# K and Q projections that write PSUM in pair order, flat copies out of PSUM, and a refitted order

## The chip, the cores and the metric

The kernel runs on one core of a Trainium2 chip. The metric is the device time of one execution in microseconds (us). The executions of one kernel mostly agree within 1%. Where a ratio is given, it is the mean time of one kernel's fast runs over the mean of the other's of the same rounds, so it is not quite the ratio of the medians quoted beside it. Of each kernel one execution was profiled.

In the profiles PE is TensorE (matmuls), PEld its weight loads, ACT ScalarE, DVE VectorE and POOL GpSimd.

## The reference, cut to what matters

```python
# x: (1, 2048, 512) bf16; 64 segments of 32 tokens, 8 memory rows carried from one to the next
for s in range(64):
    h = concat([mem, x_norm[s*32:(s+1)*32]])          # 40 rows
    q, k, v = h @ Wq, h @ Wk, h @ Wv                  # each 512 -> 32 heads x 128
    p = softmax(mask(q @ k.T * 128**-0.5))
    o = (p @ v) @ Wo                                  # 32*128 -> 512
    mem, out[s] = o[:8], o[8:]                        # the next segment needs these 8 rows
# then a residual, two layernorms and an MLP 512 -> 1792 -> 512 over all 2048 rows
```

## The kernel before: the parts that matter

The projections run as four column tiles of 32 side by side. Matmul `j` of a group writes the 512 results of 16 heads, columns `32*j` to `32*j+31` of each head, into 32 partitions of a PSUM bank. Four groups (`cc`) add up over the 512 inputs. The 32 rows are the 24 first tokens and the 8 memory rows of a segment (`hT`, "segment rows"), or the 8 last tokens of each of four segments together (`hB`, "block rows").

```python
def one_pass(lhs, reads, W, key, r, bank, rhs):
    for cc in range(DC):
        def f(e, cc=cc):
            for j in range(4):
                ins = e.matmul(ps[bank][32 * j:32 * j + 32, :], lhs(cc), rhs(W, r, cc, j), start=(cc == 0), stop=(cc == DC - 1), tile_position=(0, 32 * j))
            return ins
        S.op("pe", f, reads=[(key, r, cc)] + reads, writes=[("ps", bank)], dur=0.216, mode=MC, ni=8)

def cols_kq(W, r, cc, j):
    return W[:, cc, r * 2048:(r + 1) * 2048].rearrange("p (h e) -> p h e", h=16)[:, :, 32 * j:32 * j + 32]

def kq_out(i, bank, scale_=None):            # copy out of PSUM, to bf16
    src = ps[bank][:, :].rearrange("p (h b e) -> p h b e", b=2, e=32)
    dst = pairs(kqP[:, i, :]).rearrange("p h e b -> p h b e")
    S.either(copy2(dst, src, 512, True, scale_), reads=[("ps", bank)], writes=[("kqP", i)])

def pair_T(dst, i, key):                     # two bf16 heads transposed as one 4-byte word
    S.op("dve", lambda e: e.transpose(dst.bitcast(U32), kqP[:, i, :].bitcast(U32)), ...)
```

PSUM holds head pair `h`, head `b`, column `e` in that order. The transpose on DVE wants the two heads of a pair side by side, so the copy on ACT reads PSUM flat and writes bf16 at a step of two elements. What follows is a chain: K and Q transposed, eight Q columns copied into ZC, the score matmuls (line 771), softmax, PV, the output projection (line 884), and `hT`, the memory rows of the next segment. `ORDER` and `BANKS` give the PE order and the PSUM banks, tuned for each position of a segment in its block of four. `BONUS`, `LEAN` and the `dur=` numbers steer where a scheduler places the work of ACT, DVE and POOL at build time.

## Time and profile before

| | before |
|---|---|
| time | 877.5 us |
| busy share of the span: PE / ACT / DVE | 93% / 71% / 60% |
| PE busy between 200 and 700 us | 487.7 of 500 us |
| start to start, four K/Q column tiles of 128x512 | 216 ns (median) |
| copies of K and Q: 160 casts, 160 scaled | 740 and 757 ns |
| copies of V, same size, not stepped | 586 ns |
| period of a segment | 11.16 us |

The period is the mean distance of the transposes of `TT`, one for each segment, over 52 segments of the steady part; the start-to-start times are worked out from the starts of the matmul records.

From the page of the kernel before: the engine row (busy us, share, instructions) and the chain that ended last, by engine and by line.

```profile
PE 813.7 (93%) x22285; PEld 444.2 (51%) x22045; DVE 529.0 (60%) x1651; ACT 626.7 (71%) x1624; POOL 145.5 (17%) x353
...
PE 70%; DVE 12%; ACT 11%; DMA 3%; issue 2%; SPq 1%; POOL 0%; DVEq 0%
```

The groups of instructions of the kernel before (line, engine, operation, out<-in, shapes, count | busy us, mean ns of one | idle time of the engine just before, and what ended it):

```profile
L619 PE MATMUL ps<-WQ,hT 128*32 128x512 bf16 x2048 | 154.8, 383 | 4.7 <-DVE hT L890 4.6
L619 PE MATMUL ps<-WK,hT 128*32 128x512 bf16 x2048 | 152.4, 379 | 0.0
L619 PE MATMUL ps<-WV,hT 128*32 128x512 bf16 x2016 | 147.3, 380 | 0.0
...
L645 ACT ACTIVATE kqP<-ps 128x512 bf16<-128x512 f32 x160 | 119.4, 757 | 28.6 <-PE ps L619 27.2
L644 ACT CAST kqP<-ps 128x512 bf16<-128x512 f32 x160 | 117.0, 740 | 13.3 <-PE ps L619 10.9
...
L644 ACT CAST VS<-ps 128x512 bf16<-128x512 f32 x128 | 74.8, 586 | 2.6 <-PE ps L619 1.4
...
L771 PEld LDWEIGHTS ps<-KALL,ZC 128*32 128x32 bf16 x2048 | 25.8, 96 | 58.1 <-DVE KALL L672 51.3 <-ACT ZC L641 1.4 <-DVE QT L672 0.9
```

K, Q and V matmuls are alike, about 380 ns each. That is the recorded duration of one, whose end the profiler models; four run side by side, and a new four start every 216 ns. The K and Q copies are 154 to 171 ns longer than the V copies of the same size. The last line is the weight load for the scores: it sat idle for 51 us in all until K had been copied and transposed, but part of that idle time is hidden behind matmuls that still run. The true gaps are seen in the matmul starts: between 130 and 750 us, the gaps before the score matmuls exceed the undisturbed 216 ns by about 16.5 us in total.

One steady stretch of the chain of waits (start us, us, what):

```profile
438.91 3.48 PE ps L619 x64
442.40 0.25 PE ps L771 x13
```

64 column tiles are 16 groups of four, at 3.48 / 16 = 0.2175 us each: here the chain is nothing but PE at its rate.

### The profile page before, as it was taken

To read this page: it belongs to the slowest core of one execution; us is meant where nothing else is said; L and a number is where in the kernel's file an instruction comes from. 1 tells how busy PE (TensorE), PEld (TensorE's weight loads), DVE (VectorE), ACT (ScalarE), POOL (GpSimd) and SP (SyncE) were. 2 spreads that over 40 slices of the span, in tenths; PEclk is the share of its full clock that TensorE was granted. 3 is DMA by queue.
4 is the path that set the end of the run, shared out by engine and by line. 5 is a ranking of instruction groups with operands and counts; after the bars stand their busy time and mean duration, and the time that the engine had idled before them with its cause. 6 is when DMAs were issued, how large, how long until landed. Compare 5 with 4: busy or idle time off the path is not lost.

```text
span 878.3 us, 48583 instructions
## 1 busy us (share of the span) xinstructions
PE 813.7 (93%) x22285; PEld 444.2 (51%) x22045; DVE 529.0 (60%) x1651; ACT 626.7 (71%) x1624; POOL 145.5 (17%) x353
## 2 busy tenths in 40 slices
PE   2478999999999999999999999999999998899998
PEld 0134555555555555555555555555555554544443
DVE  2146666767676767676767676767676767442111
ACT  1348887878787878787878787878787877644442
POOL 3022111212120212121212111111111111033200
PEclk9879999999999999999999999999999999999999
DMA  8860001010101010101010101010101110501000
GB/s 339 303 210 16 4 7 31 13 32 10 35 10 29 17 28 16 28 16 29 16 28 16 28 16 28 10 28 10 28 11 28 34 28 10 198 34 49 24 25 25
DMA packets 35305, 40.48 MB, mean 46 GB/s; under 512 B 2452, under 2 KB 31004, under 8 KB 35100
## 3 DMA queue, kind: packets, MB, share of 16 engines
q1 hardware_dynamic: 35100, 37.38, 13.0%
q8 instruction: 174, 2.85, 1.3%
q14 instruction: 31, 0.25, 0.1%
HBM read 28.98 MB, written 8.39 MB: 43 GB/s over the span
## 4 chain that ended last, share of the span: by engine, by line
PE 70%; DVE 12%; ACT 11%; DMA 3%; issue 2%; SPq 1%; POOL 0%; DVEq 0%
PE ps L619 30%; PE ps L884 16%; PE ps L1162 6%; PE quad L1169 6%; PE quad L801 3%; ACT kqP L645 3%; ACT EC L783 2%; PE ps L771 2%; ACT kqP L644 2%; PE ps L631 2%; PE ps L830 2%; PE quad L856 1%; DVE PC L789 1%; PE ps L396 1%; DVE opT L912 1%
## 5 line engine op out<-in xcount | busy, mean ns | idle before, releaser
L619 PE MATMUL ps<-WQ,hT 128*32 128x512 bf16 x2048 | 154.8, 383 | 4.7 <-DVE hT L890 4.6
L619 PE MATMUL ps<-WK,hT 128*32 128x512 bf16 x2048 | 152.4, 379 | 0.0
L884 PE MATMUL ps<-WO,OT 128*32 128x256 bf16 x4224 | 141.6, 275 | 6.2 <-ACT OT L644 3.2
L619 PE MATMUL ps<-WV,hT 128*32 128x512 bf16 x2016 | 147.3, 380 | 0.0
L645 ACT ACTIVATE kqP<-ps 128x512 bf16<-128x512 f32 x160 | 119.4, 757 | 28.6 <-PE ps L619 27.2
L644 ACT CAST kqP<-ps 128x512 bf16<-128x512 f32 x160 | 117.0, 740 | 13.3 <-PE ps L619 10.9
L884 PEld LDWEIGHTS ps<-WO,OT 128*32 128x32 bf16 x4224 | 96.1, 96 | 35.9 <-ACT OT L644 17.7
L644 ACT CAST OT<-quad 128x128 bf16<-128x128 f32 (+1 forms) x192 | 85.4, 445 | 36.6 <-PE quad L805 32.9
L845 POOL TENSOR_TENSOR PA<-SA,rsa 128x256 bf16<-128x256 f32 x64 | 40.1, 627 | 379.5 <-DVE rsa L844 263.2
L896 DVE STREAM_TRANSPOSE TT<-ps 128x256 f32<-128x256 f32 x66 | 29.7, 450 | 107.3 <-PE ps L884 107.1
L619 PEld LDWEIGHTS ps<-WQ,hT 128*32 128x32 bf16 x2048 | 57.0, 97 | 59.4 <-DVE hT L890 13.9
L672 DVE STREAM_TRANSPOSE KALL<-kqP 128x256 uint32<-128x256 uint32 x160 | 70.1, 438 | 26.4 <-ACT kqP L644 24.1
L619 PEld LDWEIGHTS ps<-WK,hT 128*32 128x32 bf16 x2048 | 57.8, 97 | 54.3 <-ACT kqP L645 6.4
L783 ACT ACTIVATE EC<-ps,nmc 128x64 f32<-128x64 f32 x256 | 77.9, 309 | 8.7 <-DVE nmc L779 8.7
L1165 ACT ACTIVATE WQ<-ps,b1t 128x512 bf16<-128x512 f32 x56 | 38.5, 688 | 61.4 <-PE ps L1162 60.9
L644 ACT CAST VS<-ps 128x512 bf16<-128x512 f32 x128 | 74.8, 586 | 2.6 <-PE ps L619 1.4
L672 DVE STREAM_TRANSPOSE QT<-kqP 128x256 uint32<-128x256 uint32 x128 | 56.7, 443 | 21.9 <-ACT kqP L645 18.8
L842 ACT ACTIVATE SA<-SA 128x256 f32<-128x256 f32 x64 | 26.5, 414 | 45.3 <-DVE SA L841 43.6
L771 PEld LDWEIGHTS ps<-KALL,ZC 128*32 128x32 bf16 x2048 | 25.8, 96 | 58.1 <-DVE KALL L672 51.3
L1169 PE MATMUL quad<-WK,WQ 128*128 128x512 bf16 x224 | 54.4, 379 | 0.5 <-DVE xr L930 0.5
L1213 DVE TENSOR_TENSOR WV<-quad,WV 128x512 bf16<-128x512 f32 x16 | 11.1, 691 | 65.9 <-PE quad L1169 65.8
L642 POOL COPY ZC<-QT 128x128 bf16<-128x128 bf16 x112 | 33.0, 295 | 104.3 <-DVE QT L672 103.6
(111 smaller groups left out, 1282.3 us busy)
## 6 DMA issues: line engine op xcount, KB each, us to landing
WV<-in_A_Wv_dram SPq DMA_DIRECT2D x4, 1024.0 KB, 6.7
WK<-in_A_Wk_dram SPq DMA_DIRECT2D x4, 1024.0 KB, 8.0
v_last<-VSB SPq DMA_DIRECT2D x64, 64.0 KB, 2.1
WQ<-in_A_Wq_dram SPq DMA_DIRECT2D x4, 1024.0 KB, 8.0
VBD<-v_last SPq DMA_DIRECT2D x64, 64.0 KB
WO<-in_A_Wo_dram SPq DMA_DIRECT2D x4, 1024.0 KB, 8.9
WK<-in_B_w_dram SPq DMA_DIRECT2D x2, 1792.0 KB, 13.0
xr<-in_A_x_dram SPq DMA_DIRECT2D x16, 128.0 KB, 2.9
```

The costliest lines, as they stand in the source:

```text
L619: ins = e.matmul(ps[bank][32 * j:32 * j + 32, :], lhs(cc), rhs(W, r, cc, j), start=(cc == 0), stop=(cc == DC - 1), tile_position=(0, 32 * j))
L642: "pool": (lambda e: e.tensor_copy(out, src), t_pool(n))}
L644: return {"act": (lambda e: e.copy(out, src), t_act(n, ps_)), "dve": (lambda e: e.tensor_copy(out, src), 0.165 + 1.0e-3 * n * fast)}
L645: return {"act": (lambda e: e.mul(out, src, scale_), t_act(n, ps_)), "dve": (lambda e: e.tensor_scalar(out, src, scale_, None, ALU.mult), ...
L672: S.op("dve", lambda e: e.transpose(dst.bitcast(U32), kqP[:, i, :].bitcast(U32)), reads=[("kqP", i)], writes=[key], dur=0.445)
L771: ins = e.matmul(ps[bank][32 * j:32 * j + 32, 64 * sl:64 * sl + 64], ZC[:, par, h, :], rhs, start=False, stop=(i == 3), tile_position=(0, ...
L783: ins = e.activation(EC[:, r, sl, :], ps[bank][:, 64 * sl:64 * sl + 64], ACTF.Exp, bias=nmc[:, r, sl:sl + 1], accum_out=smc[:, r, sl:sl + 1])
L845: pa = lambda e: e.tensor_tensor(PA[:], SA[:], bc(rsa), ALU.mult)
L884: ins = e.matmul(ps[bank][32 * j:32 * j + 32, 0:256], lhs(slot(h)), wo_cols(h, b), start=(k == 0), stop=(k == 15), tile_position=(0, 32 * ...
L1162: ins = e.matmul(ps[bank][:, 0:SBT], W1[:, cc, fc * P:(fc + 1) * P], hnT_of(k)[:, cc, :], start=(cc == 0), stop=(cc == DC - 1))
L1165: S.op("act", lambda e: e.activation(gT[:, fc, :], ps[bank][:, 0:SBT], ACTF.Gelu_apprx_tanh, bias=b1t[:, fc:fc + 1], scale=1.0), reads=[(" ...
L1169: S.op("pe", lambda e: e.matmul(quad[:, t, :], gT[:, fc, t * P:(t + 1) * P], W2[:, fc, :], start=(fc == 0), stop=(fc == FC - 1)), reads=[" ...
```

## The change

The intent: let the PE put the two heads side by side, so that the copy on ACT is flat on both sides and no longer pays for its step. Three parts: the PSUM pattern of the K and Q matmuls, the flat copy, and newly fitted `ORDER`, `BANKS`, `BONUS`, `LEAN` and some `dur=` entries. The cut diff:

```diff
-BONUS = {"EC0": -2.26, "EC1": 40, ...          # all values new
+BONUS = {"EC0": 7.93, "EC1": -1.44, ...
-LEAN = 22.363
+LEAN = 15.318
-(("Q0", 0, 2), ("K0", 0, 3), ("Q0", 2, 4), ("Q1", 0, 1), ("K0", 3, 4), ("Q1", 1, 4), ("K1", 0, 4), ("SC0", 0, 1), ("V0", 0, 2), ...
+(("Q1", 0, 4), ("Q0", 0, 4), ("K0", 0, 4), ("K1", 0, 2), ("V0", 0, 1), ("K1", 2, 4), ("V1", 0, 1), ("SC0", 0, 1), ("V0", 1, 2), ...
-    dict(Q0=4, Q1=6, K0=7, K1=4, V0=7, V1=6, SC0=5, SC1=4, ...),
+    dict(Q0=5, Q1=4, K0=6, K1=4, V0=7, V1=6, SC0=5, SC1=4, ...),
 ...
+        def placer(rhs):
+            return (lambda o: o) if rhs is cols_v else (lambda o: o.rearrange("p (h e b) -> p h b e", e=32, b=2))
-    ins = e.matmul(ps[bank][32 * j:32 * j + 32, :], lhs(cc), rhs(W, r, cc, j), ...)
+    ins = e.matmul(place(ps[bank][32 * j:32 * j + 32, :]), lhs(cc), rhs(W, r, cc, j), ...)
 ...
-            return W[...].rearrange("p (h e) -> p h e", h=16)[:, :, 32 * j:32 * j + 32]
+            return W[...].rearrange("p (h b e) -> p h b e", b=2, e=E)[:, :, :, 32 * j:32 * j + 32]
 ...
-            src = ps[bank][:, :].rearrange("p (h b e) -> p h b e", b=2, e=32)
-            dst = pairs(kqP[:, i, :]).rearrange("p h e b -> p h b e")
-            S.either(copy2(dst, src, 512, True, scale_), ...)
+            S.either(copy2(kqP[:, i, :], ps[bank][:, :], 512, True, scale_), ...)
```

The moving operand is the same 512 columns in the same order. New is that two columns computed one after the other land two fp32 words (8 bytes) apart in PSUM.

## The prediction

> **What bounds the kernel now.** The page gives PE 93% busy over 878.3 us (ACT 71%, DVE 60%); in the windows from 200 to 700 us PE is busy 97 to 99%. The chain of waits from 130 to 750 us is mostly PE: the projection line (K, Q, V) 36%, the output projection 20%; the ACT copies of K and Q only 3.0% + 2.1%. In the steady part four 128x512 column tiles of a projection start every 216 ns. I summed, from the PE starts between 130 and 750 us, how far each gap exceeds the usual gap of its kind: 35 to 39 us in all. The largest item, about 16 us (0.15 us each time), is the gap before the score matmuls, which wait for the copy of K or Q, its transpose and the copy into ZC. So removing every wait could win about 4%; the rest is PE work that stays.
>
> **What the change does.**
> 1. Removed: the strided write of the K and Q copies. Groups by form: 160 casts at 740 ns and 160 scaled copies at 757 ns; the same size without stride (VS, VSB) takes 580 to 586 ns. Estimate: 320 x 0.16 = 50 us less ACT time, ACT from 71% to about 66%.
> 2. Added: the 5120 K and Q matmuls write PSUM at a step of two fp32 words. The Trainium skill, "PSUM — Partial Sum Buffer", Specifications, says that any non-contiguous pattern slows matmuls significantly (8-byte lines). No matmul of this trace writes at a step, so it cannot tell. If the rate halved, 1280 groups of four at 216 ns would cost 276 us more: about 1130 us. I think it likelier that the rate stays: the order was refitted with 0.216 us still entered for these matmuls while other entries were corrected to the trace's durations. This is the main bet.
> 3. Moved: PE order. Q comes in one block, then K, with single V units before the scores, so that the scores wait less; 30 copies into ZC go from POOL (295 ns) to ACT. PE instruction counts are the same.
>
> **How much is on the critical path.** Each segment (about 11.1 us) has four K/Q copies in a row on ACT; the score matmul waits for the last of its half. Shortening them by 0.16 us, more where they queue, should remove most of the 16 us before the scores, and the refit a part of the other 20 us; some comes back as other waits, as the loop of the memory rows is nearly as long as a segment's PE work. I expect 8 to 22 us, middle 14 us. The start (60 us) and the MLP (110 us) do not change.
>
> **Prediction.** 864 us; 80% range 848 to 886 us. Chances: faster by over 2% (below 860) 0.34, within 2% 0.46, slower by over 2% 0.20 (nearly all of it slow matmuls).
>
> **What would show it.**
> - Groups by form: K and Q copies at 580 to 600 ns, ACT near 580 us.
> - Start to start of four K/Q column tiles still 216 ns, recorded duration near 380 ns. At 430 ns step 2 is wrong.
> - Gap before the scores: from 16 to about 5 us; PE busy sum unchanged.
> - Segment period 11.1 to about 10.9 us.
>
> **What would make it wrong.** Matmuls slowed by the stepped PSUM write (far above 1000 us, or some per cent if partly); a refit that fits its model and not the chip; ACT freed where PE is the limit, so that the time stays within 1%; or a refit that removes the other waits too.

## The result, and the profile after

| | before | after |
|---|---|---|
| time | 877.5 us | 1119.1 us (1118.0 to 1120.1, two runs) |
| ratio | | 1.275 (1.270 to 1.281), slower |
| granted clock, mean | 0.986 | 0.992 |
| ACT busy | 626.7 us | 607.9 us |
| PE busy between 200 and 700 us | 487.7 us | 497.6 us |
| start to start, four K/Q column tiles | 216 ns | 429 ns |
| period of a segment | 11.16 us | 14.91 us |

The page of the changed kernel, the same rows:

```profile
PE 1068.5 (96%) x22271; PEld 510.8 (46%) x22045; DVE 535.4 (48%) x1651; ACT 607.9 (54%) x1654; POOL 137.7 (12%) x323
...
PE 90%; ACT 4%; DMA 2%; DVE 1%; SPq 1%; issue 1%; POOL 0%; POOLq 0%; DVEq 0%
```

Its groups of instructions (lines have moved by four to six):

```profile
L624 PE MATMUL ps<-WK,hT 128*32 128x512 bf16 x2048 | 252.0, 628 | 0.0
L624 PE MATMUL ps<-WQ,hT 128*32 128x512 bf16 x2048 | 237.8, 635 | 5.4 <-DVE hT L894 5.4
L624 PE MATMUL ps<-WV,hT 128*32 128x512 bf16 x2016 | 168.6, 394 | 0.0
...
L651 ACT ACTIVATE kqP<-ps 128x512 bf16<-128x512 f32 x160 | 94.0, 597 | 189.0 <-PE ps L624 189.0
L650 ACT CAST kqP<-ps 128x512 bf16<-128x512 f32 x160 | 93.8, 586 | 147.2 <-PE ps L624 147.2
```

V, which still writes flat, keeps its duration to within 4%; K and Q, on the same source line with the same sizes, go from about 380 to about 630 ns. The copies became as short as hoped (586 and 597 ns), and now wait for PE: 189 + 147 us of idle time before them, against 29 + 13 us. A stretch of the chain of waits of the changed kernel:

```profile
509.84 7.22 PE ps L624 x68
```

68 tiles are 17 groups, 7.22 / 17 = 0.425 us each (one of the 17 is a group of V). So the changed PE rate is visible before any experiment. What is not: that the step in PSUM causes it rather than the new order, the banks or the three-level patterns; and what the other parts of the change are worth.

The arithmetic nearly closes, and the rest is instructive. 1280 groups of K and Q, each 213 ns longer, are 273 us. The kernel lost 242 us. The section on the prediction works out where the other 31 us are.

### The profile page after: what moved, and what is told of

It is laid out like the page before. It is cut to its first block, busy times and chain, and to the rows that moved or that the text cites. A ratio compares the mean times of both kernels' runs of the same rounds, so it can differ in the third digit from the quotient of the medians.

```text
span 1118.4 us, 48595 instructions
## 1 busy us (share of the span) xinstructions
PE 1068.5 (96%) x22271; PEld 510.8 (46%) x22045; DVE 535.4 (48%) x1651; ACT 607.9 (54%) x1654; POOL 137.7 (12%) x323
## 4 chain that ended last, share of the span: by engine, by line
PE 90%; ACT 4%; DMA 2%; DVE 1%; SPq 1%; issue 1%; POOL 0%; POOLq 0%; DVEq 0%
PE ps L624 57%; PE ps L888 14%; PE quad L1173 4%; PE ps L1166 4%; PE quad L805 2%; PE ps L637 1%; PE ps L834 1%; PE ps L775 1%; ACT EC L787 1%; PE quad L860 1%; PE ps L397 1%; ACT kqP L650 1%; DMA WQ<-in_A_Wq_dram 1%; DMA xr<-in_A_x_dram 1%; PE quad L809 1%
## 5 line engine op out<-in xcount | busy, mean ns | idle before, releaser
L624 PE MATMUL ps<-WK,hT 128*32 128x512 bf16 x2048 | 252.0, 628 | 0.0
L624 PE MATMUL ps<-WQ,hT 128*32 128x512 bf16 x2048 | 237.8, 635 | 5.4 <-DVE hT L894 5.4
L651 ACT ACTIVATE kqP<-ps 128x512 bf16<-128x512 f32 x160 | 94.0, 597 | 189.0 <-PE ps L624 189.0
L650 ACT CAST kqP<-ps 128x512 bf16<-128x512 f32 x160 | 93.8, 586 | 147.2 <-PE ps L624 147.2
L624 PE MATMUL ps<-WV,hT 128*32 128x512 bf16 x2016 | 168.6, 394 | 0.0
L624 PEld LDWEIGHTS ps<-WV,hT 128*32 128x32 bf16 x2016 | 54.9, 108 | 48.8 <-issue 37.9
L624 PE MATMUL ps<-WQ,hB 128*32 128x512 bf16 x512 | 69.1, 620 | 4.7 <-DMA WQ<-in_A_Wq_dram 4.7
L624 PE MATMUL ps<-WK,hB 128*32 128x512 bf16 x512 | 65.6, 618 | 0.8 <-ACT VS L650 0.7
L783 DVE TENSOR_REDUCE nmc<-ps 128x2 f32<-128x128 f32 x128 | 36.4, 285 | 61.8 <-PE ps L775 60.5
L701 POOL COPY ZC<-QTB 128x256 bf16<-128x256 bf16 x64 | 25.4, 397 | 294.1 <-PE ps L775 265.4
```

The costliest lines, as they stand in the source:

```text
L624: ins = e.matmul(place(ps[bank][32 * j:32 * j + 32, :]), lhs(cc), rhs(W, r, cc, j), start=(cc == 0), stop=(cc == DC - 1), tile_position=(0 ...
L650: return {"act": (lambda e: e.copy(out, src), t_act(n, ps_)), "dve": (lambda e: e.tensor_copy(out, src), 0.165 + 1.0e-3 * n * fast)}
L651: return {"act": (lambda e: e.mul(out, src, scale_), t_act(n, ps_)), "dve": (lambda e: e.tensor_scalar(out, src, scale_, None, ALU.mult), ...
L701: S.op("pool", lambda e: e.tensor_copy(dst, src), reads=[("QTB", bk % 2, q) for q in range(2)], writes=[("ZCb", par)], dur=0.403)
L783: S.op("dve", lambda e: e.tensor_reduce(nmc[:, r, :], v, AX.X, ALU.max, negate=True), reads=[("ps", bank)], writes=[("nmc", r)], dur=0.287)
```

## The experiments

Eleven runs. Theory S: a step of two words in PSUM halves the rate of a matmul, and this is the whole loss. Rival R: the refitted order or banks cause it. A second question came out of the first batch: where the gain of about 14 us went that the prediction expected if the rate had stayed.

A warning on the comparison with the reference. All runs passed it, those with a wrong pairing of heads too. An estimate from the inputs says why: with weights of 0.05 x 512^-0.5, a row of Q or K has a spread of about 0.05, and a score about 0.05 x 0.05 = 0.0025, so the softmax is almost flat whatever K and Q hold. The check says little about these layouts here. The layouts called right below are right by construction: every value lands at the same address as before.

### 1. The new layout with the old order (old_stepped)

```diff
 # the changed kernel, with BONUS, LEAN, ORDER, BANKS and the dur= entries of the kernel before
```

> The new layout (stepped PSUM write, flat copies) with the order of the kernel before. Theory S (the step of two words in PSUM halves the rate of K and Q matmuls, whatever the order): four K or Q column tiles start every 429 ns, time 1115 to 1150 us. Rival R (the refitted order or its banks cause the loss): 216 ns and 860 to 880 us.

Measured: 1112.9 us, ratio 1.265 (1.261 to 1.269), 429 ns for four tiles. The time is 2 us below the range written down; the mechanism is as expected. The loss is there without the refit: rival R falls as the cause of it. From its page:

```profile
L623 PE MATMUL ps<-WK,hT 128*32 128x512 bf16 x2048 | 270.9, 634 | 0.0
```

### 2. The changed kernel with a flat PSUM write (new_flat)

```diff
-            return (lambda o: o) if rhs is cols_v else (lambda o: o.rearrange("p (h e b) -> p h b e", e=32, b=2))
+            return lambda o: o                # heads not paired: wrong result on purpose
```

> The changed kernel with one edit: K and Q matmuls write their 512 columns to PSUM one after the other; the copies stay flat, the order is the same instruction for instruction. The result is wrong on purpose (the columns of two heads are not paired). Theory S: 216 ns for four tiles, time 850 to 868 us, as the prediction had it for matmuls that do not slow down. Rival R (order), or that the three-level pattern of the moving operand is at fault: 1119 us stays.

Measured: 877.6 us, ratio 0.998 (0.994 to 1.002), 216 ns for four tiles. The order on ACT, DVE, POOL and the DMA queue is the same, instruction for instruction; only the PSUM pattern of the K and Q matmuls differs, and it is worth 1119.1 - 877.6 = 241.5 us. This settles the cause of the loss. The moving operand kept its three-level pattern, so that pattern is innocent. But the time is also 10 us above the range expected: even with free steps the change as a whole would have gained nothing. From its page:

```profile
L624 PE MATMUL ps<-WQ,hT 128*32 128x512 bf16 x2048 | 132.5, 385 | 9.5 <-DVE hT L894 5.4
L624 PE MATMUL ps<-WK,hT 128*32 128x512 bf16 x2048 | 140.0, 379 | 0.0
```

### 3. The refitted order alone (new_old_layout)

```diff
 # new_flat, and the copy of the kernel before:
-            S.either(copy2(kqP[:, i, :], ps[bank][:, :], 512, True, scale_), ...)
+            src = ps[bank][:, :].rearrange("p (h b e) -> p h b e", b=2, e=32)
+            dst = pairs(kqP[:, i, :]).rearrange("p h e b -> p h b e")
+            S.either(copy2(dst, src, 512, True, scale_), ...)
```

> The refitted order alone, with the layout of before (flat PSUM write, K and Q copies that write at a step, 740 to 757 ns). Right result. Theory S: 860 to 880 us, no 429 ns gaps. Rival R (order): above 1000 us. Against the flat run it tells what 0.16 us on each of 320 copies is worth on ACT.

Measured: 900.1 us, ratio 1.025 (1.020 to 1.030). The expectation was missed by 20 us: the new order makes the old layout slower, by 2.0 to 3.0%. Against new_flat, which has the same order of work, shorter copies are worth 22 us.

### 4. The pairing on the moving operand (new_read_pairs)

```diff
 # new_flat, with the columns of the moving operand read pair by pair:
-    ...rearrange("p (h b e) -> p h b e", b=2, e=E)[:, :, :, 32 * j:32 * j + 32]
+    ...rearrange("p (h b e) -> p h e b", b=2, e=E)[:, :, 32 * j:32 * j + 32, :]
```

> The pairing moved to the other operand: the moving operand is read from SBUF in the order head pair, column, head (neighbours 256 bytes apart), PSUM is written flat, the copies are flat. Right result. If only the PSUM side minds steps: 216 ns, 850 to 868 us, a version that beats both kernels. If the SBUF side minds it as much: near 429 ns or more, 1119 us or above.

Measured: 1182.9 us, ratio 1.345 (1.341 to 1.349), 482 ns for four tiles. Two neighbours of the stream that lie 256 bytes apart in SBUF cost more than two that lie 8 bytes apart in PSUM. Pairing in the PE is dear on either side. From its page:

```profile
L624 PE MATMUL ps<-WK,hT 128*32 128x512 bf16 x2048 | 275.4, 643 | 0.0
```

### 5. Flat writes and copies with the old order (old_flat)

```diff
 # old_stepped with the edit of experiment 2 (wrong result on purpose)
```

> Flat PSUM write and flat K/Q copies (result wrong on purpose: heads not paired) with the order of the kernel before. The flat run with the refitted order came to 877.6 us, no gain. Theory A (the gain of about 14 us is there, and the refit gave it back): 858 to 868 us, gap before the scores near 5 us instead of 16. Theory B (the time that ACT saves is worth nothing, as other waits take its place): 874 to 880 us.

Measured: 865.9 us, ratio 0.984 (0.982 to 0.986). So theory A holds: shorter copies under the old order gain 14 us, the prediction's middle, and the refitted order gives 12 us of them back (877.6 - 865.9). The gaps before the scores fell from 16.5 to 7.6 us between 130 and 750 us (about 5 had been written down).

### 6. The step on the read side of the copy (old_gather, and old_gather_2)

```diff
 # the kernel before, one edit: PSUM read at a step, SBUF written flat (right result)
-            src = ps[bank][:, :].rearrange("p (h b e) -> p h b e", b=2, e=32)
-            dst = pairs(kqP[:, i, :]).rearrange("p h e b -> p h b e")
+            src = ps[bank][:, :].rearrange("p (h b e) -> p h e b", b=2, e=32)
+            dst = pairs(kqP[:, i, :])
```

> The kernel before, with the step of the K/Q copies moved from the SBUF write to the PSUM read: the copy reads neighbours 32 words apart and writes flat. Right result. If a copy minds a step only on the write side: 580 to 600 ns each and the time of the flat run with the old order. If it minds the read as much: 740 ns or more and 877 us or above.

Measured: 867.5 us, ratio 0.987 (0.984 to 0.989). A later run beside other kernels:

> The kernel before with the stepped PSUM read in the copies, again, on the same chip as the two mixed kernels: 864 to 870 us, 1 to 2% faster than before, if the first result holds.

Measured: 865.1 us, ratio 0.983 (0.981 to 0.986). This edit of two lines beats both kernels, and does it with the matmuls and the order untouched. Its groups of instructions:

```profile
L645 ACT ACTIVATE kqP<-ps 128x512 bf16<-128x512 f32 x160 | 94.2, 593 | 30.7 <-PE ps L619 29.1
L644 ACT CAST kqP<-ps 128x512 bf16<-128x512 f32 x160 | 93.7, 585 | 23.3 <-PE ps L619 18.1
...
L771 PEld LDWEIGHTS ps<-KALL,ZC 128*32 128x32 bf16 x2048 | 32.6, 96 | 40.7 <-DVE KALL L672 28.2 <-ACT ZC L641 1.4 <-DVE QT L672 0.8
```

The copies take 585 and 593 ns, as if neither side had a step. The weight loads of the scores waited 28.2 us for K instead of 51.3 us. The period of a segment went from 11.16 to 10.95 us, and 64 segments of 0.21 us are 13 us, the gain measured.

### 7. The same copies with the refitted order (new_gather)

```diff
 # experiment 3 with the edit of experiment 6 (right result)
```

> The same stepped read in the copies, with the refitted order. If the read is free: 877 us as the flat run of that order; if not, 900 us as the run with the old layout.

Measured: 884.2 us, ratio 1.004 (1.001 to 1.007). It lies between the two numbers written down, nearer to the flat run (the copies take 586 and 595 ns), about 6 us above it by the ratios (1.004 against 0.998; the two ran in different batches); that difference I did not trace. The loss by the refit shows again, here with a right result.

### 8. Eight ways to write 512 words (patterns)

```diff
 # the kernel before; o is the [32, 512] output of one tile (wrong result on purpose)
-                        ins = e.matmul(o, ...)
+                        # one pattern for each of K/Q, half, segment or block rows, e.g.
+                        ins = e.matmul(o.rearrange("p (k s) -> p s k", s=2), ...)           # single words, step 2
+                        ins = e.matmul(o.rearrange("p (k s t) -> p s k t", s=2, t=2), ...)  # pairs, step 4
```

> The kernel before with eight ways of writing 512 words to PSUM, one for each of K and Q, first and second half, segments and block rows (result wrong on purpose). Theory L (the cost is one access for each 8-byte pair[...]): pairs and runs of four at a step, and runs of 32 in another order: 216 ns for four tiles; single words at a step of 2, 4 or 8: 429 ns, all alike; the order 0,2,1,3 also 429 ns, or 216 if a buffer gathers two lines. Rival P (any pattern of more than one level is slow): pairs and runs slow too. Rival B (banks inside PSUM): the cost grows with the step, more than 429 ns at step 8.

| source line | what is written one after the other | start to start, four tiles (median over the run) |
|---|---|---|
| 622 | single words, step 2 | 429 ns |
| 630 | single words, step 4 | 398 ns |
| 628 | single words, step 8 | 429 ns |
| 636 | words 0, 2, 1, 3, then 4, 6, 5, 7 | 429 ns |
| 624 | pairs, step 4 | 216 ns |
| 634 | pairs, step 8 | 226 ns |
| 632 | runs of four, step 8 | 216 ns |
| 626 | runs of 32, in another order | 216 ns |
| 638 | flat (V) | 216 ns |

The single-source views of this run, matmuls with K or Q and segment rows or block rows (count: duration ns min/median/max, first and last start):

```profile
L622 PE MATMUL ps<-WK,hT x1024: 589/634/634, 27.2 to 860.6; 128*32 128x512 bf16 x171
L624 PE MATMUL ps<-WK,hT x1024: 379/379/421, 28.9 to 863.0; 128*32 128x512 bf16 x171
L626 PE MATMUL ps<-WQ,hT x1024: 376/379/715, 44.9 to 858.7; 128*32 128x512 bf16 x171
L628 PE MATMUL ps<-WQ,hT x1024: 592/634/1142, 46.7 to 861.9; 128*32 128x512 bf16 x171
L630 PE MATMUL ps<-WK,hB x256: 590/602/634, 24.6 to 780.6; 128*32 128x512 bf16 x128
L632 PE MATMUL ps<-WK,hB x256: 379/379/421, 26.3 to 781.4; 128*32 128x512 bf16 x128
L634 PE MATMUL ps<-WQ,hB x256: 377/379/421, 32.4 to 793.4; 128*32 128x512 bf16 x128
L636 PE MATMUL ps<-WQ,hB x256: 589/634/1142, 36.8 to 794.5; 128*32 128x512 bf16 x128
```

There are two classes and nothing between: a median duration of 379 ns where the words of the stream, taken two by two, lie side by side, 602 to 634 ns where they do not. In the kernel before all these places write flat and take 216 ns, so the place is not the cause. (The 398 and 226 ns come from the few groups of block rows that follow one of their own kind, 20 each; they lie within 8% of their class.) Rival P falls, as pairs and short runs are three-level patterns and free. Rival B falls, as step 8 costs what step 2 costs. The order 0, 2, 1, 3 fills two 8-byte lines within four words and is slow all the same (429 ns), so no gathering over two lines is seen. All eight results are as theory L has them. Not shown is that the 8-byte line itself is the reason: every pair here starts at an even word, and a pair at an odd word was not tried. The run's time (989.3 us, one run, state unknown) is a sum of all eight and is not compared.

### 9. Which half of the refit costs the 12 us (oldpe_newlist, newpe_oldlist)

```diff
 # old_gather and new_gather, with ORDER and BANKS exchanged (right results)
```

> Layout with the stepped PSUM read in the copies (right result). PE order and banks of before; the priorities and durations that place the work of ACT, DVE and POOL as refitted. Theory O (the PE order and its banks cost the 12 to 17 us by which the refit loses): about 867 us, as the run with everything of before. Theory B (the placing of work on the other engines costs it): 875 to 884 us.

> The mirror image: PE order and banks as refitted, priorities and durations of before, the same stepped read in the copies. Theory O: 880 us or above. Theory B: about 867 us. If both mixed kernels are slow, order and priorities fit only together.

Measured: the old PE order with the new priorities 891.1 us (ratio 1.012, 1.010 to 1.015), the new PE order with the old priorities 906.5 us (1.029, 1.026 to 1.031). The first is 7 us above the range of its theory B, so neither number written down for it came; the second lies in the range of theory O. Both mixed kernels are slower than both matched ones (865.1 and 884.2 us): either half alone costs more (26 and 41 us) than both together (19 us), so order and priorities fit only together. Why the refitted pair as a whole is worse than the old pair stays open. What can be seen is where the time went, from the matmul starts between 130 and 750 us. In new_flat the gaps before the scores fell to 3.7 us (old_flat: 7.6), but those between projection groups rose to about 10 us (old_flat: about 2; both depend somewhat on what is taken as undisturbed). In all, a segment of new_flat is 0.19 us longer than one of old_flat (11.12 against 10.93), and 0.18 us of it lie in the time from a projection group to whatever follows it on PE. The waits of PE in new_flat show a part of this (waiting line <- releaser: us in total, times, longest):

```profile
PE ps L624 <- ACT kqP L651: 3.6, 14, 0.3
```

This line has no counterpart in the PE waits of old_flat or of the kernel before. The trace shows who waits: all 14 are Q matmuls of segment rows, one in every fourth segment, about 44 us apart. One of them, at 160.08 us, begins 0.05 us after the second of two copies of Q block rows has ended. It is the first group of `Q0`, and in the new `BANKS` `Q0` has bank 5, as has `F0`, a half of the Q block rows of the segment before; in the old `BANKS` `Q0` has bank 4. So a bank that the copy has not yet emptied is the likely reason for this wait. It is 3.6 us of some 11 us lost between 130 and 750 us, and no run tested it.

## Why the prediction was wrong

- **Step 2, the stepped PSUM write. Wrong, and this decided it.** The prediction said "I think it likelier that the rate stays" and called this "the main bet". The runs put 429 ns in place of 216 ns for four tiles, with either order, and 241.5 us on this edit alone. So the cost that was judged unlikely came in full: 213 ns of PE time for each of 1280 groups, on the engine that bounds the kernel. The evidence used was an entry of 0.216 us in a build-time model, which says what somebody assumed, not what the chip did. The Trainium skill, "PSUM — Partial Sum Buffer", Specifications, gave the warning, and the prediction quoted it and bet against it. The fallback figure was sound: 276 us for a halved rate, against 1280 x 213 ns = 273 us seen on PE.
- **The size of the loss, "about 1130 us".** Measured 1119. The period tells why it is less than 877 + 273. Of the 11.12 us of a segment in new_flat, about 0.67 us were gaps of PE (37.3 us in the 620 us between 130 and 750 us). A segment has on average 20 groups of K and Q, which add 20 x 0.213 = 4.26 us of PE work, but the period rose by only 3.79 us (11.12 to 14.91). So, by difference, 0.47 us for each segment, 30 us in 64, were gaps that got filled: while PE is slower, the copies, transposes and softmax finish in time. The matmul starts agree: from new_flat to the changed kernel the time from a projection group to what follows it rose by 4.0 us for each segment, not 4.26, and all other PE time fell by 0.2 us. The chain says little here: PE has 88% of it in new_flat and 90% in the changed kernel.
- **Step 1, shorter copies. Right in the durations, wrong in the sum.** 586 and 597 ns were predicted as 580 to 600. ACT fell to 607.9 us, not to "near 580". Thirty copies into ZC from POOL, which step 3 had named, are 9 us of the difference. For the rest, the records of ACT overlap: the sum of their durations fell by 42 us (726 to 685), but busy time counts an overlap once and fell by 19 us only.
- **Critical path: right for the copies, wrong for the refit.** "8 to 22 us, middle 14 us" was given for both together. The copies alone gave 14 us (old_flat) and 13 to 15 us (old_gather, old_gather_2). That this is just the middle is partly luck, as the middle included a gain from the refit. "The refit a part of the other 20 us" failed: the refit cost 12 us with flat PSUM writes and flat copies, 17 to 19 us with copies that read at a step, 22 us with copies that write at a step, and 6 us with stepped PSUM writes (1119.1 against 1112.9).
- **Gaps before the scores, "from 16 to about 5 us".** In new_flat 3.7 us, so the place was right; the gaps came back between the projections.
- **The range and the chances.** The case that came was given a chance of 0.20 and described as far above 1000 us, but the range ended at 886 us.

## What to carry to other kernels

When a layout must be changed on the way out of the PE, keep the matmul's two sides flat, or on the PSUM side at least in pairs of words side by side (at a step of four words they kept 216 ns), and let the copy that has to run anyway do it on its PSUM read, which cost nothing here, instead of on its SBUF write, which made it 27% longer. Before shortening an off-critical engine's work at the price of the bounding engine, time the price and the gain apart: here old_flat tells the gain (14 us), and old_stepped, which differs from it by the PSUM step alone, the price (1112.9 - 865.9 = 247 us). Test a layout and a refit of the order apart; here each hid what the other did.

## What the Trainium skill lacked or had wrong

- "PSUM — Partial Sum Buffer", Specifications, says that any non-contiguous pattern slows matmuls significantly. This is right for single words (429 ns against 216) and too wide for the rest: pairs at a step of four words, runs of four and runs of 32 kept 216 ns. "Advanced Engine Details and Errata", PSUM Cachelines, also says that every two consecutive elements should be contiguous for best throughput; that narrower sentence is the one that all eight patterns agree with. Neither page gives the factor, which was 2.0 here, nor that it does not grow with the step (2 and 8 words: both 429 ns).
- "SBUF — State Buffer", Door 1: The DMA port swizzle, the note on SBUF cachelines, says that an access which crosses to a new 16-byte line pays a penalty, without a size. The moving operand read with neighbours 256 bytes apart took 482 ns for four tiles against 216.
- The same note puts a bf16 step of up to eight elements inside what is free. The ACT copies that write SBUF at a step of two bf16 elements took 740 to 757 ns, flat ones 585 to 597 ns. No page has the cost of a stepped write by ScalarE.
- No page has it that a ScalarE copy may read PSUM with neighbours 32 words apart at no cost: 585 and 593 ns, as flat.
